# A new column layout for the transposed query weights in an agent-attention kernel with a gated convolution

## The chip, the cores and the metric

The kernel runs on one core of one Trainium2 chip. The metric is the device time of one execution in microseconds (us). The engines are called PE (TensorE, with PEld for its weight loads), DVE (VectorE), ACT (ScalarE), POOL (GpSimd) and SP (SyncE, which here issues nearly all DMAs); the profile names them so.

## The reference

Attention through 49 "agents", and on its output a gated causal convolution with two projections. There are 4 batches of N = 12800 rows with C = 128 channels, all in float32.

```
a2k     = softmax(scale * agents @ k.T)        # 49 x N
agent_v = a2k @ v                              # 49 x 128
q2a     = softmax(scale * q @ agents.T)        # N x 49
x       = q2a @ agent_v                        # N x 128
gate    = sigmoid(sum over 5 taps: conv_w[tap] * x[row - 4 + tap])
out     = ((gate * (x @ w_val)) @ w_out)
```

## The kernel before

The kernel never forms x. With the 49 query weights of a row as input, the convolution and the value projection are linear, so agent_v, conv_w and w_val are folded into small stationary matrices (`fold_weights`, five steps per batch: normalise, scale, subtract, transpose, split), one per tap for the gate and one for the values.

**Units and chunks.** A batch is cut into 10 units of 1280 rows and into 25 chunks of 512. Per unit, `key_scores`, `agent_values` and `queries` run; per chunk, `gates`, `values` and `project`.

**Precision.** Matmuls on the transposed weights run in f16. To keep float32 accuracy each weight w and each stationary value s is held as a high part and a rest (w = w_hi + w_lo, s = s_hi + s_lo), and the products hi*hi, lo*hi and hi*lo are added up by contraction over partitions: the columns of one matmul carry several copies of the 49 weights. 49 low parts, 49 high parts and 30 of the high parts once more (to meet the rests of s) fill 128 columns. The other 19 high parts that have to meet rests of s have no column left; they go into a second tile, x2.

**From weights to x1.** `queries` ends with `qw` (128 rows x 10 blocks x 49 weights, float32; L772). ACT casts it to the high parts (L779), POOL copies 30 of them again (L784) and subtracts to get the low parts (L794); all land in `pt` (128 x 10 x 128, f16). Then `transposes` turns `pt` around: for the first four units on PE (L849) with copies by ACT and DVE (L856, L861), for the other 36 by a DMA transpose (L835) that SP issues. The result is a half of an `x1` tile: 128 partitions (one per column of `pt`) by 2560 positions, two units to a tile, with the last four positions of the tile before in front of it (`halo`, on POOL, L816 and L819).

**From x1 to x2.** `shifts` (L884) copies 19 partitions of x1 into x2, each five times, shifted by 0 to 4 positions (the taps): 95 partitions. It does so by two transfers of SP's queue, one of 15 rows that lie three partitions apart and one of 4 neighbours; once per unit for the first four units, later once for two units (5 KB a row). For each chunk, `gates` runs five matmuls on x1 (one per tap, L922) and one on x2 (L926); `values` runs one on x1 (L949) and one on x2 (L953); then `project` runs three (L992 to L994). Between them stand a tanh on ACT (L935), a product on DVE (L962, `h`), the split of `h` on ACT (L968, `hh`) and POOL (L973, `hl`), and the scaled output on ACT (L1006).

**Order.** Every step is entered into a `Plan` with an engine, an estimated duration and its keys for reading and writing. PE runs in the order that a text written out by hand gives (`order`); the other engines' order, SP's queue among them, comes out of a list scheduling with the estimated durations. So each engine works in a fixed order, and a late step holds up all that stands behind it on its engine. Loads of k, q and v go through 11 buffers (`ld`), outputs through 4 (`ob`), `pt` through 4, x1 through 4 and x2 through 3.

The names of the layout before are these:

```
THREES = 15
NDUP = 2 * THREES
X2R = 19
X2CUTS = ((0, THREES, 3, 0.5), (THREES, X2R, 1, 0.3))
```

## Time and profile before

| | us |
|---|---|
| three timed runs | 424.02, 425.49, 425.74 |
| their median | 425.49 |
| span of the profiled execution (first to last instruction) | 423.6 |
| PE busy in it | 403.9 (95%) |
| ACT, DVE, POOL busy | 301.5, 293.3, 228.2 |
| mean granted clock of PE | 0.985 |

The profile is that of an execution of its own, whose time stands in the table only as its span; what lies around the span (the start and the end of an execution) and the spread from run to run make up the difference to the runs. In its rows a line such as L922 is a line of the kernel above, `out<-in` are the names of tiles without their numbers, so that `x` stands for x1 and x2 alike: `x<-pt` is the transpose into x1, `x<-x` the pair of transfers from x1 into x2. A wait names who waited, and for whom.

### The profile page before, as it was taken

What the parts mean: (1) busy time and instruction counts of PE and PEld (TensorE: products, weight loads), DVE (VectorE), ACT (ScalarE), POOL (GpSimd) and SP (SyncE); (2) the same over time, 40 slices, a digit from 0 to 9 for tenths busy, and PEclk for the clock granted to TensorE, in tenths of its full rate; (3) what the DMA queues carried; (4) which work ended last, traced back from release to release, by engine and by line L of the source; (5) the groups of instructions that cost most, each with busy time, mean ns of one, the idle gap of its engine ahead of it and who ended that gap; (6) DMA issues with size and microseconds to landing.
All of it is one profiled execution on the core that took longest, in us unless ns stands there. A gap on an engine that the chain in (4) does not pass through costs nothing.

```text
span 423.6 us, 10042 instructions
## 1 busy us (share of the span) xinstructions
PE 403.9 (95%) x3907; PEld 197.0 (47%) x3907; DVE 293.3 (69%) x562; ACT 301.5 (71%) x521; POOL 228.2 (54%) x263
## 2 busy tenths in 40 slices
PE   4979999999999999999999899999999989999995
PEld 1358434346555443446555343335555534344443
DVE  3757899867875978667795575767765678676231
ACT  1564568779966777678876486778876567788776
POOL 1002557654657565554566355574366277877553
PEclk9969999999999999999999899999999999999998
DMA  8999999999999999999999999999999977755733
GB/s 320 420 417 411 370 367 353 301 295 310 412 293 283 346 317 362 304 278 356 351 379 324 271 299 370 314 332 302 296 393 322 239 196 161 199 163 176 205 121 124
DMA packets 75129, 127.62 MB, mean 301 GB/s; under 512 B 50466, under 2 KB 50850, under 8 KB 75084
## 3 DMA queue, kind: packets, MB, share of 16 engines
q1 hardware_dynamic: 74940, 126.87, 96.9%
q8 instruction: 30, 0.49, 0.5%
q10 hardware_dynamic: 144, 0.13, 0.2%
q14 instruction: 15, 0.12, 0.1%
HBM read 79.25 MB, written 26.21 MB: 249 GB/s over the span
## 4 chain that ended last, share of the span: by engine, by line
PE 78%; DMA 9%; DVE 8%; ACT 1%; POOL 1%; issue 1%; SPq 0%; POOLq 0%; DVEq 0%; ACTq 0%
PE gate L922 23%; PE sc L376 17%; PE av L480 10%; PE val L949 5%; PE out L992 5%; PE val L953 5%; PE gate L926 5%; PE out L993 4%; DMA ld<-kT 4%; PE out L994 4%; DMA x<-pt 3%; DMA x<-x 2%; DVE h L962 1%; DVE qw L772 1%; DVE qsm L763 1%
## 5 line engine op out<-in xcount | busy, mean ns | idle before, releaser
L973 POOL TENSOR_TENSOR hl<-h,hh 128x512 f16<-128x512 f32 (+1 forms) x101 | 116.9, 1158 | 96.1 <-ACT hh L968 96.0
L922 PE MATMUL gate<-x,stat 128*128 128x512 f16 (+1 forms) x500 | 125.2, 380 | 0.2 <-ACT th L935 0.2
L962 DVE SCALAR_TENSOR_TENSOR h<-th,val 128x512 f32<-128x512 f32 x100 | 67.8, 678 | 66.8 <-PE out L993 26.2
L376 PE MATMUL sc<-ld,ag_sb 128*32 128x320 f32 x1280 | 101.5, 447 | 7.6 <-DMA ld<-kT 7.0
L935 ACT ACTIVATE th<-gate,unscale 128x512 f32<-128x512 f32 x100 | 68.3, 683 | 33.3 <-PE gate L926 31.7
L1006 ACT ACTIVATE ob<-out,oscale 128x512 f32<-128x512 f32 x98 | 67.3, 687 | 21.3 <-PE out L994 20.1
L922 PEld LDWEIGHTS <-stat 128*128 128x128 f16 x505 | 46.3, 97 | 63.7 <-issue 14.8
L968 ACT CAST hh<-h 128x512 f16<-128x512 f32 (+1 forms) x101 | 61.5, 609 | 17.2 <-DVE h L962 16.4
L750 POOL TENSOR_TENSOR qw<-sT,qmx 128x490 f32<-128x490 f32 x40 | 41.4, 1035 | 47.6 <-DVE qmx L745 47.5
L376 PEld LDWEIGHTS sc<-ld,ag_sb 128*32 128x32 f32 x1280 | 36.7, 111 | 59.4 <-issue 25.7
L480 PE MATMUL av<-ld,eT 128*32 128x129 f32 (+1 forms) x1400 | 50.7, 279 | 1.0 <-DVE eT L386 1.0
L480 PEld LDWEIGHTS av<-ld,eT 128*32 128x32 f32 (+1 forms) x1400 | 47.1, 117 | 7.5 <-issue 2.5
L794 POOL TENSOR_TENSOR pt<-qw,pt 128x490 f16<-128x490 f32 x40 | 44.8, 1120 | 3.1 <-ACT pt L779 2.9
L471 ACT ACTIVATE e<-ks,kbias 128x320 f32<-128x320 f32 x80 | 39.3, 554 | 5.4 <-DVE eT L386 3.3
L386 DVE STREAM_TRANSPOSE sT<-sc 128x640 f32<-128x640 f32 x40 | 33.6, 839 | 13.4 <-PE sc L376 12.7
L402 ACT COPY ks<-sc 128x640 f32<-128x640 f32 x40 | 27.7, 691 | 21.2 <-PE sc L376 19.1
L386 DVE STREAM_TRANSPOSE eT<-e 128x640 f32<-128x640 f32 x40 | 33.5, 842 | 9.8 <-ACT e L471 5.2
L926 PE MATMUL gate<-x,stat 95*128 95x512 f16 x100 | 38.3, 383 | 1.5 <-DMA x<-x 1.5
L949 PE MATMUL val<-x,stat 128*128 128x512 f16 x100 | 38.2, 382 | 0.8 <-DVE h L962 0.6
L953 PE MATMUL val<-x,stat 95*128 95x512 f16 x100 | 38.1, 381 | 0.0
L994 PE MATMUL out<-hl,wo 128*128 128x512 f16 x98 | 37.0, 378 | 1.1 <-POOL hl L973 1.1
L992 PE MATMUL out<-hh,wo 128*128 128x512 f16 x98 | 37.3, 381 | 0.1
(130 smaller groups left out, 389.4 us busy)
## 6 DMA issues: line engine op xcount, KB each, us to landing
ld<-kT SPq DMA_DIRECT2D x40, 640.0 KB
ld<-qT SPq DMA_DIRECT2D x40, 640.0 KB
ld<-vP SPq DMA_DIRECT2D x39, 645.0 KB
outT<-ob SPq DMA_DIRECT2D x48, 512.0 KB
x<-x SPq DMA_DIRECT2D x18, 375.0 KB
x<-x SPq DMA_DIRECT2D x18, 100.0 KB
outT<-ob SPq DMA_DIRECT2D x3, 256.0 KB
x<-x SPq DMA_DIRECT2D x4, 187.5 KB
```

What stands on the lines that cost most here:

```text
L376: nc.tensor.matmul(out=out[g * BLK : (g + 1) * BLK, j, 0:GT], lhsT=ag_sb[:, b, j * BLK : (j + 1) * BLK], rhs=src[:, g * GT : (g + 1) * GT] ...
L386: nc.vector.transpose(out=out.rearrange("p n (j i) -> p j n i", j=2), in_=in_.rearrange("p j (n i) -> p j n i", i=BLK),)
L480: nc.tensor.matmul(out=av[o + j : o + j + cols, 0 : C + 1], lhsT=et[:, n, j : j + cols], rhs=vt[:, n, :], start=(u == 0 and n < 2), stop=( ...
L922: nc.tensor.matmul(out=pg, lhsT=stat[:, k, :], rhs=x1[:, c : c + w], start=(k == 0), stop=False,)
L926: nc.tensor.matmul(out=pg, lhsT=stat[0 : TAPS * X2R, TAPS + 1, :], rhs=x2[0 : TAPS * X2R, o2 : o2 + w], start=False, stop=True,)
L935: lambda: nc.scalar.activation(out=th, in_=pg, func=AF.Tanh, scale=unscale[:, 0:1]),
L949: nc.tensor.matmul(out=pv, lhsT=stat[:, TAPS, :], rhs=x1s[(b * NCH + n0 // CH) // 5 % NX][:, PAD + o2 : PAD + o2 + w], start=True, stop=False,
L953: nc.tensor.matmul(out=pv, lhsT=stat[0 : TAPS * X2R, TAPS + 2, :], rhs=x2[0 : TAPS * X2R, o2 : o2 + w], start=False, stop=True,)
L962: lambda: nc.vector.scalar_tensor_tensor(out=h, in0=th, scalar=1.0, in1=pv, op0=ALU.add, op1=ALU.mult),
L968: "act", 0.16 + 0.42 * scale, lambda: nc.scalar.copy(out=hh, in_=h),
L973: lambda: nc.gpsimd.tensor_tensor(out=hl, in0=h, in1=hh, op=ALU.subtract),
L1006: lambda: nc.scalar.activation(out=ob[:, o : o + w], in_=po, func=AF.Copy, scale=oscale),
```

## The change

The columns of `pt` get a new layout. The high parts lie first at every fourth column: of columns 32 to 99, column 32 + 4i + r holds weight 16r + i for r = 0, 1, 2 and i = 0 to 16 (weights 16 and 32 stand there twice); the fourth slot, r = 3, holds a second copy of 16 of the weights, and column 99 is the first of 17 low parts. The other 32 low parts fill columns 0 to 31, and columns 116 to 127 hold 12 more second copies. x2 then takes its 19 rows from partitions 32, 36, ..., 92 (16 rows) and 85, 89, 93 (3 rows), and fills its own partitions 24 to 118; its other partitions are set to zero once, and the matmuls on x2 read all 128 partitions instead of 95. The stationary matrices are laid out to match.

On the engines this means:

- ACT writes the high parts with a step of four columns, 510 elements a row instead of 490 (two weights twice).
- POOL writes the second copies by two instructions (160 and 120 elements) instead of one (300), and the low parts by two (320 and 170) instead of one (490).
- In `fold_weights` the rests are made by five subtractions (values: three before, gate: four before), and ACT copies the high parts by four instructions instead of two.
- Three instructions on POOL clear x2 at the start.
- The estimates in the plan change a little (ACT 0.58 to 0.6; POOL 0.44 to 0.5 and 1.09 to 1.15), so that some steps change places.

PE's instructions keep their order. On DVE, the value part of the first batch's fold before (`wst` is the folded matrix, `sT` the next unit's transposed scores):

```order
L597 TENSOR_SCALAR wst_124<-val,rs 128x49
L582 SCALAR_TENSOR_TENSOR wst_124<-val,rs,wst_124 128x30
L582 SCALAR_TENSOR_TENSOR wst_124<-val,rs,wst_124 128x15
L582 SCALAR_TENSOR_TENSOR wst_124<-val,rs,wst_124 128x4
L386 STREAM_TRANSPOSE sT_86<-sc_135 128x2x10x32
```

and the same place on DVE in the changed kernel:

```order
L640 TENSOR_SCALAR wst_124<-val,rs 128x3x17
L624 SCALAR_TENSOR_TENSOR wst_124<-val,rs,wst_124 128x16
L624 SCALAR_TENSOR_TENSOR wst_124<-val,rs,wst_124 128x12
L624 SCALAR_TENSOR_TENSOR wst_124<-val,rs,wst_124 128x2
L624 SCALAR_TENSOR_TENSOR wst_124<-val,rs,wst_124 128x16
L624 SCALAR_TENSOR_TENSOR wst_124<-val,rs,wst_124 128x3
L406 STREAM_TRANSPOSE sT_86<-sc_135 128x2x10x32
```

Two subtractions more stand ahead of `sT`. On POOL, at the weights of units 18 and 19 (`pt_99` and `pt_100`) before:

```order
L794 TENSOR_TENSOR pt_99<-qw_91,pt_99 128x10x49
L973 TENSOR_TENSOR hl_117<-h_111,hh_114 128x512
L794 TENSOR_TENSOR pt_100<-qw_92,pt_100 128x10x49
L784 TENSOR_SCALAR pt_100<-qw_92 128x10x30
L750 TENSOR_TENSOR qw_90<-sT_86,qmx_88 128x490
L973 TENSOR_TENSOR hl_118<-h_112,hh_115 128x512
```

and there now:

```order
L821 TENSOR_TENSOR pt_99<-qw_91,pt_99 128x10x32
L826 TENSOR_TENSOR pt_99<-qw_91,pt_99 128x10x17
L1006 TENSOR_TENSOR hl_117<-h_111,hh_114 128x512
L821 TENSOR_TENSOR pt_100<-qw_92,pt_100 128x10x32
L826 TENSOR_TENSOR pt_100<-qw_92,pt_100 128x10x17
L813 TENSOR_SCALAR pt_100<-qw_92 128x10x16
L813 TENSOR_SCALAR pt_100<-qw_92 128x10x12
L777 TENSOR_TENSOR qw_90<-sT_86,qmx_88 128x490
L1006 TENSOR_TENSOR hl_118<-h_112,hh_115 128x512
```

Each instruction on `pt` has become two; the steps stand in the same order. On SP, the same units' transposes and their pair of transfers into x2 (here `x_105`, from `x_1_102`) before:

```order
L835 DMA_TRANSPOSE x_1_102<-pt_99 128x10x128
L369 DMA ld_71<-kT 128x1280
L835 DMA_TRANSPOSE x_1_102<-pt_100 128x10x128
L1021 DMA outT<-ob_123 128x1024
L369 DMA ld_61<-kT 128x1280
L369 DMA ld_62<-qT 128x1280
L884 DMA x_105<-x_1_102 75x1x2560
L884 DMA x_105<-x_1_102 20x1x2560
```

and now:

```order
L869 DMA_TRANSPOSE x_1_102<-pt_99 128x10x128
L389 DMA ld_71<-kT 128x1280
L869 DMA_TRANSPOSE x_1_102<-pt_100 128x10x128
L1054 DMA outT<-ob_123 128x1024
L389 DMA ld_61<-kT 128x1280
L389 DMA ld_62<-qT 128x1280
L917 DMA x_105<-x_1_102 80x1x2560
L917 DMA x_105<-x_1_102 15x1x2560
```

Nothing has moved there; the pair is cut 80 and 15 instead of 75 and 20. On SP, places are changed at one earlier spot (an output and a load) and within the work for units 23 to 29; on POOL and ACT at several, mostly the two parts of `pt` against each other and against `hl`.

The core of the diff:

```diff
-THREES = 15
-NDUP = 2 * THREES
+HI = 32
+FOURS = 17
+RUN = 16
+LO1 = HI + 4 * FOURS - 1
+TWICE = 12
 X2R = 19
-X2CUTS = ((0, THREES, 3, 0.5), (THREES, X2R, 1, 0.3))
+X2O = 24
+X2CUTS = ((0, RUN, HI, 0.5), (RUN, X2R, HI + 53, 0.3))
+
+
+def highs(x):
+
+
+    if len(x.shape) == 2:
+        return x[:, HI : HI + 4 * FOURS].rearrange("p (i r) -> p r i", r=4)
+    return x[:, :, HI : HI + 4 * FOURS].rearrange("p k (i r) -> p k r i", r=4)
+
+
+def overlapped(x):
+
+    ap = [tuple(d) for d in x.ap]
+    return bass.AP(x.tensor, x.offset, ap[:-1] + [(RUN, 3), (1, FOURS)])
...
+    for t in x2s:
+        nc.gpsimd.memset(t, 0.0)
...
-        def rest(out, full, s, hi):
-            dve.scalar_tensor_tensor(
-                out=out, in0=full, scalar=rs[:, s : s + 1], in1=hi,
-                op0=ALU.mult, op1=ALU.subtract,
-            )
...
+            less(pick(out, slice(HI + 3, HI + 4 * RUN, 4)), pick(full, slice(2 * RUN + 1, A)), pick(hi, 2, slice(1, FOURS)))
+            less(pick(out, slice(P - TWICE, P)), pick(full, slice(RUN + 1, RUN + 1 + TWICE)), pick(hi, 1, slice(1, 1 + TWICE)))
+            less(pick(out, slice(HI + 4 * RUN, HI + 4 * RUN + 2)), pick(two, slice(0, 2), 0), pick(hi, slice(1, 3), 0))
+            less(x2_(slice(0, RUN)), pick(full, slice(0, RUN)), pick(hi, 0, slice(0, RUN)))
+            less(x2_(slice(RUN, X2R)), pick(full, slice(2 * RUN - 3, 2 * RUN)), pick(hi, 1, slice(RUN - 3, RUN)))
...
+            nc.scalar.copy(
+                out=wg[:, :, 0:HI].rearrange("p k (r i) -> p k r i", i=RUN), in_=hi[:, :, 0:2, 0:RUN]
+            )
+            nc.scalar.copy(out=wg[:, :, LO1 : LO1 + FOURS], in_=hi[:, :, 2, :])
...
-        add(
-            "act", 0.58, lambda: nc.scalar.copy(out=pt[:, :, A : 2 * A], in_=w),
+        hi = highs(pt)
+        add(
+            "act", 0.6, lambda: nc.scalar.copy(out=hi[:, :, 0:3], in_=overlapped(w)),
             [("qw", g % NPT)], [(*p_, 0)],
         )
...
+        def again():
+            for to, a0, n in ((pt[:, :, HI + 3 : HI + 4 * RUN : 4], 2 * RUN + 1, RUN), (pt[:, :, P - TWICE :], RUN + 1, TWICE)):
+                nc.gpsimd.tensor_scalar(
+                    out=to, in0=w[:, :, a0 : a0 + n], scalar1=1.0, scalar2=0.0,
+                    op0=ALU.mult, op1=ALU.add,
+                )
+
+        add("pool", 0.5, again, [("qw", g % NPT)], [(*p_, 2)])
+
+        def lows_():
+            nc.gpsimd.tensor_tensor(
+                out=pt[:, :, 0:HI].rearrange("p n (r i) -> p n r i", i=RUN),
+                in0=w[:, :, 0:HI].rearrange("p n (r i) -> p n r i", i=RUN),
+                in1=hi[:, :, 0:2, 0:RUN], op=ALU.subtract,
+            )
+            nc.gpsimd.tensor_tensor(
+                out=pt[:, :, LO1 : LO1 + FOURS], in0=w[:, :, HI:A], in1=hi[:, :, 2, :],
+                op=ALU.subtract,
+            )
+
+        add("pool", 1.15, lows_, [("qw", g % NPT), (*p_, 0)], [(*p_, 1)])
...
-        for r0, r1, every, us in X2CUTS:
-            first = A + (2 if every == 3 else 3 * THREES)
-            rows = x1[first : first + 1 + (r1 - r0 - 1) * every : every, c : c + 1]
+        for r0, r1, first, us in X2CUTS:
+            rows = x1[first : first + 1 + (r1 - r0 - 1) * 4 : 4, c : c + 1]
             view = [rows.ap[0], (1, TAPS), (1, n * UNIT)]
             add(
                 "dma", 0.6,
                 lambda r0=r0, r1=r1, rows=rows, view=view: nc.sync.dma_start(
-                    out=x2[r0 * TAPS : r1 * TAPS, o : o + n * UNIT],
+                    out=x2[X2O + r0 * TAPS : X2O + r1 * TAPS, o : o + n * UNIT],
...
             nc.tensor.matmul(
-                out=pg, lhsT=stat[0 : TAPS * X2R, TAPS + 1, :],
-                rhs=x2[0 : TAPS * X2R, o2 : o2 + w], start=False, stop=True,
+                out=pg, lhsT=stat[:, TAPS + 1, :], rhs=x2[:, o2 : o2 + w],
+                start=False, stop=True,
             )
...
             nc.tensor.matmul(
-                out=pv, lhsT=stat[0 : TAPS * X2R, TAPS + 2, :],
-                rhs=x2[0 : TAPS * X2R, o2 : o2 + w], start=False, stop=True,
+                out=pv, lhsT=stat[:, TAPS + 2, :], rhs=x2[:, o2 : o2 + w],
+                start=False, stop=True,
             )
```

77 lines of the change are left out of this document (30 added, 47 removed).

## The prediction

> **What bounds the kernel now.** I read the page first, then who waits for whom on the matmul engine, then busy time by stretches, the chain of work that ended last, the DMA views and last the groups of instructions by shape. The page's first lines, and from the busy times by stretches two spans of the run:
>
> ```profile
> span 423.6 us, 10042 instructions
> PE 403.9 (95%) x3907; PEld 197.0 (47%) x3907; DVE 293.3 (69%) x562; ACT 301.5 (71%) x521; POOL 228.2 (54%) x263
> 60.00:412.00 352.00, 348.57 (x3295) 164.52 (x3294) 249.28 (x467) 265.15 (x458) 209.38 (x230) 1.00 1.00 293
> ```
>
> In the third row the columns are the stretch, its length, and busy time of PE, PEld, DVE, ACT and POOL, then the granted clock, the DMA share and GB/s. From 60 to 412 us TensorE is idle for 352.00 - 348.57 = 3.4 us. So a change off TensorE can win back about that, plus what an idle gap costs afterwards, and no more. The waits of TensorE in that stretch (who, for whom, us in total, times, longest):
>
> ```profile
> PE gate L926 <- DMA x<-x: 1.5, 1, 1.5
> PE out L994 <- POOL hl L973: 1.1, 1, 1.1
> PE val L949 <- DVE h L962: 0.6, 1, 0.6
> ```
>
> The first is the one that the change touches: `x<-x` is the pair of transfers that fills x2, and L926 the matmul that reads x2. It waits once in the whole run. The chain of work tells where, with start, duration and what:
>
> ```profile
> 220.73 7.50 DMA x<-pt
> 228.28 7.34 DMA x<-x
> 236.89 2.24 PE gate L922 x5
> ...
> 243.56 1.19 PE gate L922 x5
> ```
>
> A transpose by DMA (`x<-pt`) is followed at once by the pair, which lands at 228.28 + 7.34 = 235.62, and TensorE goes on. But its next five gate matmuls take 2.24 us, against 1.19 seven microseconds later. The stretches around it show why:
>
> ```profile
> 234.00:236.00 2.00, 0.51 (x3) 0.21 (x3) 1.05 (x3) 0.32 (x1) 0.10 (x1) 1.00 0.66 137
> 237.00:240.00 3.00, 3.00 (x8) 1.03 (x7) 1.99 (x7) 0.96 (x2) 1.65 (x3) 0.50 1.04 327
> 240.00:243.00 3.00, 3.00 (x34) 1.56 (x36) 2.24 (x9) 1.67 (x4) 0.76 (x3) 0.93 0.96 310
> ```
>
> After 1.5 us of idle TensorE the granted clock is 0.50 for 3 us and 0.93 for the next three: 3 x 0.50 + 3 x 0.07 = 1.7 us of matmul work lost while TensorE counts as busy. This one wait costs 1.5 + 1.7 = 3.2 us.
>
> [...]
>
> **What the change does to the transfers.** The pair still moves 95 rows of 5 KB; only which partitions are read and written changes (15 rows three apart plus 4 neighbours become 16 rows four apart plus 3, and the target moves from partitions 0-94 to 24-118). What the DMA engines do with such packets shows where nothing else runs. First a stretch with loads alone (6 to 14 us), then one in which one pair is the only transfer until its end (398.58 to 401.65 us); the second row of each is packets, MB and the share of 16 engines:
>
> ```profile
> DMA packets 735, 3.35 MB, mean 419 GB/s; under 512 B 80, under 2 KB 80, under 8 KB 735
> q1 hardware_dynamic: 735, 3.35, 101.4%
> ```
>
> ```profile
> DMA packets 112, 0.49 MB, mean 158 GB/s; under 512 B 17, under 2 KB 17, under 8 KB 112
> q1 hardware_dynamic: 112, 0.49, 56.1%
> ```
>
> Loads: 1.014 x 16 x 8 us over 735 - 80 = 655 big packets is 0.198 us each. The pair: 0.561 x 16 x 3.07 us over 112 - 17 = 95 packets is 0.290 us each, though no other transfer is there. So the packets of the pair hinder each other, and what differs from a load is which partitions they touch. Best case: 95 x 0.198 / 16 = 1.2 us for what takes 3.07 now; worst case: no change. I take 2.2 us, about half way, since the writes still fall on rows that are close together, so 0.9 us is gained on a pair with nothing beside it.
>
> [...]
>
> Under load the gain comes with a second one. The DMA engines are full between 60 and 340 us, and SyncE is held while it pushes. The queue between 60 and 340 us:
>
> ```profile
> q1 hardware_dynamic: 55788, 90.06, 107.7%
> ```
>
> Two pushes of transposes (start, duration):
>
> ```profile
> 212.77 7.23 SPq L835 DMA_TRANSPOSE x<-pt  x1
> 220.73 2.63 SPq L835 DMA_TRANSPOSE x<-pt  x1
> ```
>
> And one late in the run, with little traffic:
>
> ```profile
> 392.53 1.66 SPq L835 DMA_TRANSPOSE x<-pt  x1
> ```
>
> A push that takes 1.66 us when there is room took 7.23 here, and the second transpose, on which the pair waits, could start only after it. The pair before this one lies in that queue, so its gain arrives here as well: another 0.9 us at most, 0.5 taken. Needed are 1.5 us. I count 0.9 + 0.5, plus the 0.5 us by which TensorE comes later from the start (below), less 0.4 for the later copy on POOL, if none of it hides behind the held queue: 1.5 to 1.9. So the wait just goes, and with it the half clock: **-3.2 us**. Bounds: 0 if the pair gets no faster; above zero it is +0.7, the largest later copy, since no other step ahead of the pair grows.
>
> The second wait of TensorE (1.1 us, for POOL `hl`) has a DMA behind it too; in order of time, in brackets the idle time ahead and what ended it:
>
> ```profile
> 338.78 0.19 POOL L819 COPY x<-x 128x4 f16<-128x4 f16 x1 [5.99 <-DMA x<-pt]
> ```
>
> ```profile
> 340.13 0.38 PE L994 MATMUL out<-hl,wo 128*128 128x512 f16 x1 [1.11 <-POOL hl L973]
> ```
>
> That copy (the halo) waits 6.0 us until a transpose has landed, and the `hl` for which TensorE waits stands behind it on POOL. A less full DMA queue brings that forward a little: **-0.3 us**, between 0 and -1.1.
>
> **What it adds on the other engines.** Rows by shape (count, busy us, mean ns, idle before):
>
> ```profile
> L973 POOL TENSOR_TENSOR hl<-h,hh 128x512 f16<-128x512 f32 x99 | 115.5, 1168 | 94.8 <-ACT hh L968 94.7
> L973 POOL TENSOR_TENSOR hl<-h,hh 128x256 f16<-128x256 f32 x2 | 1.3, 671 | 1.3 <-ACT hh L968 1.3
> L794 POOL TENSOR_TENSOR pt<-qw,pt 128x490 f16<-128x490 f32 x40 | 44.8, 1120 | 3.1 <-ACT pt L779 2.9
> L784 POOL TENSOR_SCALAR pt<-qw 128x300 f16<-128x300 f32 x40 | 18.2, 457 | 20.6 <-DVE qw L772 20.6
> L616 POOL TENSOR_TENSOR wst<-gs,wst 128x75 f16<-128x75 f32 x3 | 1.1, 403 | 0.5 <-ACT wst L637 0.5
> L750 POOL TENSOR_TENSOR qw<-sT,qmx 128x490 f32<-128x490 f32 x40 | 41.4, 1035 | 47.6 <-DVE qmx L745 47.5
> L779 ACT CAST pt<-qw 128x490 f16<-128x490 f32 x40 | 23.9, 600 | 10.7 <-DVE qw L772 10.7
> L271 POOL MEMSET wst<- 128x256 f16 x2 | 0.6, 312 | 0.0
> L922 PE MATMUL gate<-x,stat 128*128 128x512 f16 x495 | 124.5, 381 | 0.2 <-ACT th L935 0.2
> L926 PE MATMUL gate<-x,stat 95*128 95x512 f16 x99 | 38.0, 384 | 1.5 <-DMA x<-x 1.5
> ```
>
> - POOL, per unit: L973's two sizes give 1.94 ns an element plus 174 ns. One subtraction of 490 (1120) becomes 320 and 170 elements: 795 + 504 = 1299. L616, which reads and writes with a step, takes 403 for 75 elements where that line gives 320, a quarter more: 1299 x 1.26 = 1637. One copy of 300 becomes two of 160 and 120: one more fixed cost, 0.17 as above. Together +0.35 to +0.7 us; I take 0.45, nearer to L973, which has L794's long rows. Forty units make 18 us on an engine that is busy 228 of 424: cover enough. Without that cover it is the slow rival below.
> - ACT, per unit: 510 instead of 490 elements, so 600 x 510 / 490 = 624 at most if the fixed part grew too. No row shows ACT writing every fourth element; a subtraction on POOL loses a quarter to its step (above), so the other end is +0.15. I take +0.02. ACT is idle for 29%.
> - Matmuls that read 95 rows (L926) last 384 ns, those that read 128 (L922) 381: filling up x2 costs nothing there.
> - Clearing three x2 at the start: 2560 columns, ten times the 312 ns of L271, 3 x 3.1 = 9.4 us on POOL. The first L750 has a long idle time ahead of it, so this is hidden; without that cover TensorE would wait up to 9 us:
>
> ```profile
> 35.26 1.02 POOL L750 TENSOR_TENSOR qw<-sT,qmx 128x490 f32<-128x490 f32 x1 [32.94 <-DVE qmx L745]
> ```
>
> The folding of the weights is longer: five subtractions for three on DVE for the value weights, five for four for the gate weights, and four copies for two on ACT. In the first batch this is where TensorE does wait. From the order of time around 44 to 52 us:
>
> ```profile
> 44.33 0.53 DVE L582 SCALAR_TENSOR_TENSOR wst<-val,rs,wst 128x30 f16<-128x30 f32 x3
> 44.77 0.84 DVE L386 STREAM_TRANSPOSE sT<-sc 128x640 f32<-128x640 f32 x1
> ...
> 52.07 0.72 PE L849 MATMUL sc<-ident,pt 128*128 128x128 f16 x10 [0.52 <-DVE sT L386]
> ```
>
> Three subtractions take 0.53, so two more take 0.35; `sT` stands right behind them on DVE, and DVE's row goes on to the next `sT`, for which TensorE waits at 52.07. POOL's subtractions beside it (five for four) and the first longer copy do not add to that wait but can outlast it. I take **+0.5 us** (0.2 to 0.9; a gain is excluded, since instructions only come in). In the later batches TensorE has other work then; only the fold at 345 us has a wait near it (L949, 0.6): **+0.1 us** (0 to 0.7).
>
> Sum: -3.2 - 0.3 + 0.5 + 0.1 = -2.9 us. On the profiled span of 423.6 that is 420.7. The runs took 424.02 to 425.74 with a median of 425.49, 1.9 over the span (start and end of an execution, and spread between runs); I carry the difference over: 425.5 - 2.9 = **422.6 us**.
>
> **The rivals.** (1) The pair lands no sooner. [...] Against it: the pair alone takes 0.290 us a packet. Then the wait and the half clock stay, and only the costs count: 425.5 + 0.5 + 0.1 = 426.1, up to 426.8 if the later copies push the wait out by 0.7. [...]
>
> (2) Slower: POOL comes late with `hl`. TensorE's last projection matmul (L994) waits for `hl`, which would queue behind the longer copies. The work comes in bursts, and POOL is fullest here (the row's fifth busy time):
>
> ```profile
> 360.00:380.00 20.00, 20.00 (x115) 8.29 (x117) 13.74 (x25) 16.45 (x29) 17.03 (x18) 1.00 0.70 192
> ```
>
> It is busy 17.0 of 20 us. Forty units in some 350 us are two to three in such a stretch, so 18 to 19 then; it is full from 1.0 us more a unit on, and that is where this rival decides. If `hl` is late by 0.4 us in half of the ten units of the last batch that is 2 us, and one gap of 1.5 us brings a half clock again, 1.7: 425.5 + 0.6 + 2 to 3.7 = 428.1 to 429.8, with the wait for the pair still there (without it the case ends at 424.9 to 426.6, among the unchanged).
>
> (3) More comes free: the wait at 340 us goes whole (-1.1) and the costs at the start stay at their low end: 425.5 - 3.2 - 1.1 + 0.2 = 421.4, or 420.6 with the rest of the 3.4 us of idle time (0.8) as well.
>
> **How the numbers follow.** Forecast 0.47, no sooner 0.27, slower 0.17, more 0.09. The forecast's own range is 421.6 to 424.2, from the bounds of its terms (a part of the wait left over at the upper end). From 420.6 to 427.6 the range takes in these, the first rival and the last, and leaves out the second, 0.17. A measurement of this kernel tells about 0.5% from no change, which is 2.1 us: below 423.4 is faster. Most of the forecast and all of the last case lie there, 0.53; the rest of the forecast and most of the first rival are the same, 0.30; the second rival is slower, 0.17.
>
> **What would show it.** In the profile after: the packets of a lone pair at 0.20 to 0.25 us instead of 0.290; no wait of the x2 matmul for a DMA, and a granted clock of 1.00 from 237 to 240 us; POOL busy at 243 to 256 us; TensorE some 0.5 us later at 60 us. Wrong would be: the pair as slow as before (rival 1), or TensorE waiting for POOL `hl` in many places after 340 us (rival 2).

## The result, and the profile after

The changed kernel takes **430.57 us** (median of 8 runs, 428.97 to 431.38). The kernel before took 425.97 in 8 runs beside it. The ratio is **1.0089, 95% interval 1.0061 to 1.0118**: 0.9% slower. (The quotient of the two medians is 1.0108, inside that interval; every ratio in this text is the one on record, with its interval.) The forecast was 422.6, and the time lies above its range of 420.6 to 427.6.

The first lines of the page of the kernel after (span; busy time of each engine):

```profile
span 428.2 us, 10150 instructions
PE 403.3 (94%) x3907; PEld 196.0 (46%) x3907; DVE 299.3 (70%) x573; ACT 327.4 (76%) x529; POOL 256.1 (60%) x347
```

TensorE runs the same 3907 matmuls. ACT is busy for 25.9 us more (301.5 before), POOL for 27.9 more. The groups of the kernel after, by shape, name the places (mean of one is the number ahead of the second bar):

```profile
L807 ACT CAST pt<-qw 128x510 f16<-128x510 f32 x40 | 56.8, 1427 | 13.2 <-DVE qw L799 12.8
L821 POOL TENSOR_TENSOR pt<-qw,pt 128x320 f16<-128x320 f32 x40 | 35.8, 896 | 12.8 <-ACT pt L807 12.4
L813 POOL TENSOR_SCALAR pt<-qw 128x160 f16<-128x160 f32 x40 | 23.0, 574 | 25.0 <-DVE qw L799 22.5 <-PE gate L959 1.7 <-PE out L1026 0.7
L826 POOL TENSOR_TENSOR pt<-qw,pt 128x170 f16<-128x170 f32 x40 | 22.8, 569 | 0.0
L813 POOL TENSOR_SCALAR pt<-qw 128x120 f16<-128x120 f32 x40 | 11.8, 294 | 0.0
L959 PE MATMUL gate<-x,stat 128*128 128x512 f16 x99 | 37.5, 379 | 0.0
```

The cast of `pt` took 600 ns for 490 elements and takes 1427 for 510. (Forty times this difference is 33 us, and ACT's total grew by less: in the profile the row of an instruction can begin before the one ahead of it has ended; the cast at 58.96 us lasts 1.46 and the next row of ACT begins at 60.14.) POOL's four pieces add up to 2.33 us a unit, against 1.58. POOL now waits 12.4 us for the cast, where it waited 2.9. L959, the matmul that reads x2, no longer waits for a DMA: that part came as forecast. Who TensorE does wait for, in the kernel after:

```profile
PE sc L883 <- POOL pt L826: 2.6, 2, 1.4
PE gate L955 <- ACT th L968: 2.2, 7, 0.8
```

Both are new in this size (0.2 us each before). Two stretches, of the kernel before first (length, then busy time of PE, PEld, DVE, ACT, POOL, then clock and DMA):

```profile
40.00:70.00 30.00, 28.02 (x293) 12.70 (x289) 26.64 (x62) 18.69 (x33) 17.72 (x25) 1.00 1.02 367
70.00:412.00 342.00, 338.57 (x3210) 159.99 (x3203) 239.62 (x449) 256.76 (x444) 203.06 (x223) 1.00 0.99 291
```

The same of the kernel after, and the place where the half clock was, and the stretch in which POOL is fullest:

```profile
40.00:70.00 30.00, 24.85 (x263) 11.18 (x264) 24.73 (x61) 18.54 (x30) 16.88 (x31) 1.00 0.97 365
70.00:412.00 342.00, 336.89 (x3207) 158.78 (x3206) 242.36 (x461) 278.91 (x449) 223.21 (x296) 1.00 0.94 289
237.00:240.00 3.00, 2.99 (x17) 1.60 (x16) 1.20 (x4) 1.95 (x3) 2.67 (x4) 1.00 0.91 274
360.00:380.00 20.00, 19.66 (x112) 7.98 (x109) 13.93 (x25) 17.06 (x25) 17.96 (x26) 1.00 0.57 166
```

Between 40 and 70 us TensorE works 3.2 us less than before, and between 70 and 412 another 1.7 less (the granted clock from 20 to 40 us, which bears on the first stretch, as e_order shows below, is 0.83 in both profiles), although the wait for x2 and its half clock (0.50 from 237 to 240 us before, 1.00 now) are gone from there. The first wait for POOL's `pt`, with the chain that leads to it, in order of time:

```profile
39.29 1.40 ACT L807 CAST pt<-qw 128x510 f16<-128x510 f32 x1 [2.19 <-DVE qw L799]
40.77 0.87 POOL L821 TENSOR_TENSOR pt<-qw,pt 128x320 f16<-128x320 f32 x1 [0.77 <-ACT pt L807]
41.61 0.56 POOL L826 TENSOR_TENSOR pt<-qw,pt 128x170 f16<-128x170 f32 x1
42.22 0.73 PE L883 MATMUL sc<-ident,pt 128*128 128x128 f16 x10 [1.26 <-POOL pt L826]
```

The weights are ready at 39.29; ACT casts them, POOL waits 0.77 us for that cast and then subtracts twice, and TensorE waits 1.26 us for POOL. The cast is half of that chain.

### The profile page after: what moved, and what is told of

Read it like the earlier page. It is cut to its first block, busy times and chain, and to the rows that moved or that the text cites. A ratio compares the mean times of both kernels' runs of the same rounds, so it can differ in the third digit from the quotient of the medians.

```text
span 428.2 us, 10150 instructions
## 1 busy us (share of the span) xinstructions
PE 403.3 (94%) x3907; PEld 196.0 (46%) x3907; DVE 299.3 (70%) x573; ACT 327.4 (76%) x529; POOL 256.1 (60%) x347
## 4 chain that ended last, share of the span: by engine, by line
PE 56%; DVE 15%; ACT 13%; POOL 7%; DMA 4%; issue 4%; SPq 0%; POOLq 0%; DVEq 0%; ACTq 0%
PE gate L955 16%; PE sc L396 11%; PE av L500 9%; ACT pt L807 4%; DMA ld<-kT 4%; PE out L1025 3%; PE val L982 3%; PE out L1026 3%; PE val L986 3%; PE gate L959 3%; PE out L1027 3%; DVE h L995 3%; DVE qw L799 2%; ACT th L968 2%; POOL pt L821 2%
## 5 line engine op out<-in xcount | busy, mean ns | idle before, releaser
L807 ACT CAST pt<-qw 128x510 f16<-128x510 f32 x40 | 56.8, 1427 | 13.2 <-DVE qw L799 12.8
L821 POOL TENSOR_TENSOR pt<-qw,pt 128x320 f16<-128x320 f32 x40 | 35.8, 896 | 12.8 <-ACT pt L807 12.4
L813 POOL TENSOR_SCALAR pt<-qw 128x160 f16<-128x160 f32 x80 | 27.5, 434 | 25.0 <-DVE qw L799 22.5
L959 PE MATMUL gate<-x,stat 128*128 128x512 f16 x100 | 37.8, 378 | 0.0
```

The lines of the kernel that those rows point to most:

```text
L807: "act", 0.6, lambda: nc.scalar.copy(out=hi[:, :, 0:3], in_=overlapped(w)),
L959: nc.tensor.matmul(out=pg, lhsT=stat[:, TAPS + 1, :], rhs=x2[:, o2 : o2 + w], start=False, stop=True,)
```

## The experiments

Each ratio is against the kernel before, timed beside it, with its 95% interval. Theory A: the cast on ACT, which writes every fourth column in three passes, makes the loss; the transfers are a gain as forecast. Rivals: B, POOL's longer work; C, the longer fold of the weights or another order of the planner; and, once more, that the transfers gain nothing.

| run | what it is | ratio | interval |
|---|---|---|---|
| e_dma | before + new transfers | 0.9895 | 0.9863 to 0.9928 |
| e_act | before + a row of 0.8 us of cast ahead of the cast | 1.0035 | 1.0003 to 1.0068 |
| e_pool | before + POOL's longer work | 1.0028 | 0.9999 to 1.0056 |
| e_three | these three together | 0.9972 | 0.9951 to 0.9994 |
| e_order | after, cast in column order | 0.9934 | 0.9909 to 0.9960 |
| e_start | e_order, old cast in units 0 to 3 | 0.9971 | 0.9947 to 0.9996 |
| e_late | e_order + POOL copy in the chain | 1.0090 | 1.0056 to 1.0123 |
| e_half | e_order + 0.56 us cast behind the cast | 0.9975 | 0.9951 to 0.9999 |
| e_load | e_order + 0.93 us cast behind the cast | 1.0108 | 1.0078 to 1.0139 |
| e_flat | e_order + 0.92 us cast without a step | 1.0185 | 1.0146 to 1.0224 |
| e_bload | before + the second cast of e_load | 1.0068 | 1.0040 to 1.0096 |
| e_fold | e_order, fold in column order too | 0.9936 | 0.9911 to 0.9960 |
| e_plain4 | no steps, 13 + 6 rows four apart | 1.0004 | 0.9977 to 1.0031 |
| e_plain3 | no steps, 16 rows three apart + 3 | 0.9939 | 0.9906 to 0.9971 |

**The parts alone.** First the transfers, on the old columns, so that x2 gets other rows than its weights belong to. Of each edit the core is shown, and `...` marks lines that are left out:

```
+X2CUTS = ((0, 16, 32, 0.5), (16, X2R, 85, 0.3))
...
-        for r0, r1, every, us in X2CUTS:
-            first = A + (2 if every == 3 else 3 * THREES)
-            rows = x1[first : first + 1 + (r1 - r0 - 1) * every : every, c : c + 1]
+        for r0, r1, first, us in X2CUTS:
+            rows = x1[first : first + 1 + (r1 - r0 - 1) * 4 : 4, c : c + 1]
```

> The kernel before with the new transfers alone: 16 rows four partitions apart and 3 more, x2 on partitions 24 to 118 and cleared at the start, x2's matmuls over 128 rows. The columns stay as they were, so x2 gets other rows than its weights belong to (that part of the computation is changed). Theory A (the transfers give what was forecast, and the cast on ACT takes more than that away again): 3 us less than the kernel before, ratio 0.990 to 0.995, no wait of the x2 matmul for a DMA and no half clock around 237 us. Theory C (the transfers themselves, or the order that the planner then finds, are worse): 1.000 or above, with new waits of TensorE for a DMA.

It gave 0.9895: 1.05% of 425.5 is 4.5 us, between 3.1 and 5.8, against the 3.5 of the two terms in the forecast. TensorE's waits for `hl` and for the pair in it, and where the second of them is:

```profile
PE out L996 <- POOL hl L975: 0.9, 1, 0.9
PE gate L928 <- DMA x<-x: 0.5, 1, 0.5
49.63 0.38 PE L928 MATMUL gate<-x,stat 128*128 128x512 f16 x1 [0.49 <-DMA x<-x]
```

The wait of 1.5 us for the pair at 235 us is gone, and so is the half clock behind it (1.00 from 237 to 240 us). The 0.5 us is another wait, at 49.63 us, where the kernel before has none. Of the 1.1 for `hl` 0.9 is left. So the gain was there, and the whole loss of the change is near 2% (1.0089 / 0.9895 = 1.0196, 8 us).

Next one more cast on ACT, ahead of the cast of `pt`:

```
+            nc.scalar.copy(
+                out=idle16[:, :, 0:68].rearrange("p n (i r) -> p n r i", r=4)[:, 0:5, 0:3],
+                in_=bass.AP(w.tensor, w.offset, [tuple(w.ap[0]), (A, 5), (16, 3), (1, 17)]),
+            )
             nc.scalar.copy(out=pt[:, :, A : 2 * A], in_=w)
```

> The kernel before with one more cast on ACT ahead of each unit's cast of pt: 255 elements into scratch, written at every fourth column, which took 812 ns in the weights' fold of the kernel after. So ACT's part of the pt chain grows from 600 to about 1410 ns, as in the kernel after (1427), and all else stays. Theory A (the long cast makes the loss): ratio 1.008 to 1.015, since the whole loss beside a gain of 3 us would be some 7 us. Theory B (the longer work on POOL makes it): 1.000 to 1.003.

And POOL's longer work alone (the subtraction in columns 0 to 31 and 32 to 48, and a copy of 42 columns, which stands in the part left out):

```
...
+            for a0, a1 in ((0, 32), (32, A)):
+                nc.gpsimd.tensor_tensor(
+                    out=pt[:, :, a0:a1], in0=w[:, :, a0:a1], in1=pt[:, :, A + a0 : A + a1],
+                    op=ALU.subtract,
+                )
```

> The kernel before with POOL's work on each unit lengthened to what the kernel after shows: the subtraction in two pieces of 32 and 17 columns, and one more copy of 420 elements into scratch, some 0.7 us a unit (1.58 us before, 2.33 after). ACT's cast stays at 600 ns. Theory A: ratio 1.000 to 1.004, POOL waits less for ACT than it now does. Theory B (POOL's longer work makes the loss): 1.008 to 1.015, with waits of TensorE for POOL pt or hl.

Neither is near 1.02: 1.0035 and 1.0028, the second not told from no change. Theory A had asked for 1.008 or more, so it had failed in this form. But e_act had not lengthened ACT's work as far as it meant to. Its first unit:

```profile
38.22 0.81 ACT L781 CAST idle<-qw 128x255 f16<-128x255 f32 x1 [2.19 <-DVE qw L773]
38.76 0.68 ACT L785 CAST pt<-qw 128x490 f16<-128x490 f32 x1
```

The second row begins 0.54 us after the first. From the start of the one to the end of the other are 1.22 us, where the changed kernel's cast takes 1.43, and ACT is busy for 322.0 us in all, where the changed kernel has 327.4. All three edits together (e_dma's, e_act's and e_pool's lines in one kernel):

> The kernel before with three parts at once, each of which has run alone: the new transfers (x2 gets other rows than its weights belong to, so that part of the computation is changed), the long cast on ACT (one more of 255 elements into scratch) and the longer work on POOL (two subtractions, one more copy of 420 elements into scratch). The fold and the columns of pt stay as before. If the three add up: 0.9895 x 1.0035 x 1.0028 = 0.996. Theory D (ACT and POOL stand in one chain, so that together they cost far more than each): 1.004 to 1.010, near the kernel after. Theory C (the missing part is in the fold or the order): about 0.996.

0.9972: the parts add up (0.9957 expected) and do not reach 1.0089; ACT and POOL in one chain do not cost far more together than each alone. What they had imitated was not all of it (ACT has 321.7 us here), and only an edit to the changed kernel itself could tell why.

**How the cast writes.** The next kernel copied a tile into scratch at the start, in ten forms, here (4) and (5):

```
+        go(src([(64, 10), (1, 3), (4, 16)], pout), src([(49, 10), (16, 3), (1, 16)]))
+        go(src([(64, 10), (4, 16), (1, 3)], pout), src([(49, 10), (1, 16), (16, 3)]))
```

> The kernel before with copies of one tile into scratch at the start, ten forms in this order on ACT twice, then on DVE and on POOL: (1) 480 elements, contiguous, f32 to f16; (2) 480, every second f16 written; (3) 480, three of every four f16 written in order, source contiguous; (4) 480, every fourth f16 written, three passes (the form of the kernel after); (5) the same places as in (4) but written in the order of the columns, source stepping by 16; (6) target contiguous, source stepping by 16; (7) 640, target contiguous, source in overlapping runs of four; (8) as (4) with an f32 target; (9) as (4) with every second f16; (10) as (4) with every eighth f16. Theory A1 (the distance between written elements costs, from 8 bytes on): (1), (2), (6), (7), (9) about 0.6 to 0.8 us on ACT, (4), (10) about 1.4, (5) and (3) in between or as (4). Theory A2 (what costs is the source's step of 64 bytes or the short runs): (5), (6) slow and (4) fast. Theory A3 (only f16 written in part costs): (8) fast where (4) is slow.

ACT's copies in order of time (start, duration); the first is contiguous, the second form (4), the third form (5), the last form (10). ACT ran all ten twice, with durations that agree to 0.01 us:

```profile
3.90 0.60 ACT L284 CAST pout<-qw 128x480 f16<-128x480 f32 x1 [1.48 <-DVE pout L278]
5.92 1.25 ACT L284 CAST pout<-qw 128x480 f16<-128x480 f32 x1
7.19 0.74 ACT L284 CAST pout<-qw 128x480 f16<-128x480 f32 x1
11.01 2.32 ACT L284 CAST pout<-qw 128x480 f16<-128x480 f32 x1
```

The same 480 places cost 1.25 us in three passes of every fourth column and 0.74 in the order of the columns. Every second f16 cost 0.78, every eighth 2.32; an f32 target with the same step in elements 1.04; a source with a step of 16 and a contiguous target 0.73. So A1 holds for the f16 targets, and (5) costs no more than its source's step does alone: what counts there is how far apart two writes are that follow each other. The distance in bytes does not explain all: 16 bytes apart took 2.32 us in f16 and 1.04 in f32, and no run has an f32 target without a step beside it.

That gives an edit of the changed kernel that touches nothing but the order of writing inside one instruction:

```
-            "act", 0.6, lambda: nc.scalar.copy(out=hi[:, :, 0:3], in_=overlapped(w)),
+            "act", 0.6, lambda: nc.scalar.copy(
+                out=pt[:, :, HI : HI + 4 * FOURS].rearrange("p n (i r) -> p n i r", r=4)[:, :, :, 0:3],
+                in_=bass.AP(w.tensor, w.offset, [tuple(w.ap[0]), (A, NBLK), (1, FOURS), (RUN, 3)]),
+            ),
```

> The kernel after, with the same elements of pt written by the same cast on ACT, but in the order of the columns (17 groups of three) instead of three passes that write every fourth column. On the scratch tile 480 elements took 743 ns in this order and 1245 in three passes, so the cast should take 790 ns instead of 1427; nothing else changes. Theory A (the write order of this cast is the main cost): 0.992 to 0.998 against the kernel before, most of the way from 1.009 to the 0.9895 of the transfers alone; the waits of TensorE for POOL pt at 42 and 54 us shrink by 0.6 us each, those for ACT th go. Theory B (POOL's longer work, which stays): 1.003 to 1.006. Theory C (the fold's longer instructions at the start or the planner's order): 1.005 to 1.009.

**0.9934**: faster than both kernels. Its cast, and its two stretches:

```profile
L807 ACT CAST pt<-qw 128x510 f16<-128x510 f32 x40 | 31.4, 788 | 14.3 <-DVE qw L799 14.0
```

```profile
40.00:70.00 30.00, 27.78 (x289) 12.28 (x288) 27.23 (x63) 19.15 (x34) 18.36 (x31) 1.00 1.02 377
70.00:412.00 342.00, 339.70 (x3221) 161.53 (x3220) 243.02 (x460) 264.53 (x455) 224.15 (x295) 1.00 0.96 290
```

639 ns less in one instruction a unit is worth 1.0089 / 0.9934 = 1.0156, 6.6 us. TensorE works 2.9 us more between 40 and 70 us and 2.8 more after that than in the changed kernel. Not all of the 2.9 is the cast's. From 20 to 40 us the granted clock differs between these two executions; here the changed kernel, e_order, and e_fold (below), which has the same cast as e_order:

```profile
20.00:40.00 20.00, 16.97 (x234) 14.86 (x234) 13.76 (x23) 12.30 (x24) 1.67 (x3) 0.83 1.02 416
20.00:40.00 20.00, 16.68 (x237) 12.85 (x229) 13.76 (x23) 11.90 (x24) 3.10 (x5) 0.91 1.02 414
20.00:40.00 20.00, 16.78 (x238) 14.87 (x234) 13.78 (x23) 12.19 (x24) 1.34 (x2) 0.83 1.02 415
```

and e_fold's first stretch:

```profile
40.00:70.00 30.00, 26.91 (x281) 12.07 (x278) 26.19 (x62) 17.83 (x32) 19.05 (x33) 1.00 1.02 374
```

At the clock of 0.83 the cast in order is worth 26.91 - 24.85 = 2.1 us there. The planner's costs, POOL's instructions and the fold are those of the changed kernel, so with the cast in order all that B and C still cost, and the 0.19 us that the cast is still longer than before, is what separates this kernel from the transfers alone: 0.4%, which the two intervals do not tell from nothing.

**Why 0.64 us cost so much.** At the start:

> The kernel after with the cast of pt in three passes (1427 ns) in the first four units only, whose transposes run on TensorE, and in the order of the columns in the other 36. In the profile of the kernel after TensorE waits there 2.6 us for POOL pt, in that of the ordered kernel 0.4. If the loss arises there: 0.9934 + 0.005 = 0.998 to 1.000; the other 36 units then hold the remaining 1.0 per cent. If the loss lies all in the later units: 0.993 to 0.995; if all in the first: 1.006 to 1.010.

```
+            if g < PE_FIRST:
+                nc.scalar.copy(out=hi[:, :, 0:3], in_=overlapped(w))
+                return
```

0.9971, so by the ratios 0.37% or 1.6 us arise in the first four units; the two intervals leave it just clear of nothing. Its first stretch is that of the changed kernel again, at the same clock of 0.83 from 20 to 40 us:

```profile
40.00:70.00 30.00, 25.00 (x264) 11.31 (x265) 24.72 (x61) 18.53 (x30) 16.99 (x30) 1.00 0.99 365
```

For the other 36 units, two kernels were to separate ACT's time from the length of the chain. The first puts a second cast behind the ordered one, for which nothing waits:

```
+            nc.scalar.copy(
+                out=idle16[:, :, 0:68].rearrange("p n (i r) -> p n r i", r=4)[:, 0:6, 0:3],
+                in_=bass.AP(w.tensor, w.offset, [tuple(w.ap[0]), (A, 6), (RUN, 3), (1, FOURS)]),
+            )
```

> The kernel after with the cast of pt in the order of the columns (780 ns, alone it gave 0.9934), and behind that cast one more on ACT, 306 elements into scratch with every fourth f16 written, for which nothing waits. ACT is busy as long as in the kernel after (about 1.4 us a unit), but the chain from the weights through ACT and POOL to the transposes stays 0.6 us shorter. Theory A1 (the loss comes from the chain's length): 0.993 to 0.997. Theory A2 (it comes from ACT's load: gate, ks, hh and out stand behind the cast): 1.003 to 1.010.

1.0108. The first stretch is unharmed here (27.65 us against e_order's 27.78, both with 0.91 from 20 to 40 us), and the loss comes after it, with more waits for `th`, the tanh that stands behind the casts on ACT:

```profile
40.00:70.00 30.00, 27.65 (x287) 12.45 (x287) 26.93 (x63) 20.80 (x36) 18.61 (x32) 1.00 1.02 375
70.00:412.00 342.00, 334.30 (x3186) 157.67 (x3183) 239.16 (x457) 281.30 (x481) 220.17 (x292) 1.00 0.97 288
```

```profile
PE gate L967 <- ACT th L980: 3.6, 8, 1.0
```

The second lengthens the chain and leaves ACT alone, but it gives POOL 24 us more (280.3 against 256.3):

```
         def lows_():
+            nc.gpsimd.tensor_scalar(
+                out=idle16[:, :, 0:50], in0=pt[:, :, HI : HI + 50], scalar1=1.0, scalar2=0.0,
+                op0=ALU.mult, op1=ALU.add,
+            )
```

> The kernel after with the cast of pt in the order of the columns, and between it and the subtractions one copy of 500 elements on POOL that reads what the cast wrote, some 0.5 to 0.6 us. The chain is about as long as in the kernel after, ACT's load is not. Theory A1 (the chain's length): 1.003 to 1.010. Theory A2 (ACT's load): 0.993 to 0.997, or 1.000 if POOL's own load, now 2.9 us a unit, begins to count.

1.0090. Here the first stretch is hit (24.90 us of TensorE, against e_fold's 26.91, both with 0.83 from 20 to 40 us), and later TensorE waits for POOL:

```profile
40.00:70.00 30.00, 24.90 (x264) 11.23 (x265) 24.69 (x61) 16.30 (x29) 19.25 (x34) 1.00 0.97 365
70.00:412.00 342.00, 336.15 (x3209) 159.05 (x3208) 244.93 (x461) 260.91 (x450) 245.24 (x332) 1.00 0.97 290
```

```profile
PE out L1035 <- POOL hl L1014: 2.0, 2, 1.3
```

So either costs about as much as the stepped cast did, and I had set them up as if only one could. In the first four units it is the chain: a second cast behind the first does no harm there. Later e_late does not tell the chain's length from POOL's own longer work, and the changed kernel's waits are those of e_load (`th`, 7 times) and not those of e_late (`hl`).

Three more kernels asked what in ACT's second cast costs. A row of about the same length without a step (920 ns against 930), against e_load:

```
-                out=idle16[:, :, 0:68].rearrange("p n (i r) -> p n r i", r=4)[:, 0:6, 0:3],
-                in_=bass.AP(w.tensor, w.offset, [tuple(w.ap[0]), (A, 6), (RUN, 3), (1, FOURS)]),
+                out=idle16[:, :, 0:87],
+                in_=bass.AP(w.tensor, w.offset, [tuple(w.ap[0]), (40, NBLK), (1, 87)]),
```

> As e_load, but the second cast on ACT writes 870 elements into scratch without a gap, which should take about as long (930 ns) as the 306 stepped ones. Theory A2 (ACT's time is what costs, not how it writes): 1.008 to 1.013 as e_load, with waits of TensorE for ACT th. Theory S (a stepped write slows other engines down): 0.994 to 1.000.

1.0185: without a step it costs no less, so it is not the stepped writing that harms the other engines; ACT's time does. That it costs more than forecast goes with ACT's total, which is 4.4 us above e_load's. Half of the stepped cast, against e_load (its source is cut in the same way):

```
-                out=idle16[:, :, 0:68].rearrange("p n (i r) -> p n r i", r=4)[:, 0:6, 0:3],
+                out=idle16[:, :, 0:68].rearrange("p n (i r) -> p n r i", r=4)[:, 0:3, 0:3],
```

> As e_load, with 153 instead of 306 elements in the second cast, so about half of its time on ACT beyond the fixed part. If the cost is proportional to ACT's time: 1.002 to 1.004 (half way between 0.9934 and 1.0108). If it only starts when ACT is nearly full (above some 325 us in all): 0.993 to 0.998.

0.9975. With ACT's busy time from the pages: 307.1 us (e_order) 0.9934, 319.8 (e_half) 0.9975, 332.7 (e_load) 1.0108, 337.1 (e_flat) 1.0185. The first 12.7 us cost 0.4%, the next 12.9 cost 1.3%, the last 4.4 cost 0.8% (within its interval the rate of the step before): a microsecond on ACT cost more here where ACT had more to do. e_three, built from the kernel before, fits in (321.7 us, 0.9972). The changed kernel has 327.4 us; on a straight line between e_half and e_load that gives an estimate of 1.0053, and with the 0.37% of the first four units 1.009, where 1.0089 was measured. The second cast of e_load behind the cast of the kernel before:

```
             nc.scalar.copy(out=pt[:, :, A : 2 * A], in_=w)
+            nc.scalar.copy(
+                out=idle16[:, :, 0:68].rearrange("p n (i r) -> p n r i", r=4)[:, 0:6, 0:3],
+                in_=bass.AP(w.tensor, w.offset, [tuple(w.ap[0]), (A, 6), (16, 3), (1, 17)]),
+            )
```

> The kernel before with the second cast of e_load (306 stepped elements into scratch) behind its own cast of pt. Theory A2 (ACT's time): 1.008 to 1.017 as the step from the ordered kernel to e_load. If it counts only together with POOL's longer work and the new transfers: 1.000 to 1.005, near the 1.0035 of the shorter second cast that ran ahead of the cast of pt.

1.0068 with ACT at 327.0 us, between the two forecasts, and a smaller step than from e_order to e_load. It still waits 2.4 us for `x<-x`, and such a wait can cover some of ACT's lateness; that is argued, not shown.

**The rest of the change.** The fold's high parts written in column order, in three places on DVE and ACT (`in_cols` and `cols` swap the two dimensions as in e_order):

```
-            dve.tensor_scalar_mul(vhi[:, 0:3], overlapped(pv[:, 0:A]), rs[:, 1:2])
+            dve.tensor_scalar_mul(in_cols(vhi), cols(pv[:, 0:A]), rs[:, 1:2])
-            dve.tensor_scalar_mul(ghi[:, :, 0:3], overlapped(gw), rs[:, 0:1])
+            dve.tensor_scalar_mul(in_cols(ghi), cols(gw), rs[:, 0:1])
-            add("act", 0.4, lambda: nc.scalar.copy(out=ghi[:, :, 0:3], in_=overlapped(gs)), ["gs"], [(*w_, "g")])
+            add("act", 0.4, lambda: nc.scalar.copy(out=in_cols(ghi), in_=cols(gs)), ["gs"], [(*w_, "g")])
```

> The kernel after with the cast of pt in the order of the columns, and the same for the three writes of the weights' high parts in the fold (ACT 255 elements, 812 ns in three passes, DVE 255 and 51 elements, 832 and 340 ns). Expected by the scratch copies: 812 becomes about 430 ns, and DVE's 832 about 560. If the fold holds a part of what separates the ordered kernel (0.9934) from the transfers alone (0.9895): 0.991 to 0.993, TensorE does not wait for POOL wst at 44 us. If it is hidden: 0.9934.

0.9936 against 0.9934: the stepped writes of the fold cost nothing that shows. Its added instructions were not tried alone.

Two kernels without any stepped write in the cast, with other rows for x2; the copies and the fold follow, and POOL gets one more short copy a unit (0.2 to 0.3 us):

```
-X2CUTS = ((0, THREES, 3, 0.5), (THREES, X2R, 1, 0.3))
+X2CUTS = ((0, 13, 49, 4, 0.4), (13, X2R, 51, 4, 0.3))
```

> A complete kernel that writes everything in runs as before (49 columns of the rests, 49 of the weights, 30 copies) and gets rows four apart by choosing others for x2: weights 0, 4, ... 48 (13 rows) and 2, 6, ... 22 (6 rows), to partitions 24 to 118. ACT's cast stays at 600 ns, POOL has one more copy (60 elements, some 0.2 us a unit). Theory A: 0.988 to 0.993, as the transfers alone. If the number of rows (16 and 3) matters for the transfers and not their distance: 0.995 to 1.000, with a wait of TensorE for x<-x.

```
-X2CUTS = ((0, THREES, 3, 0.5), (THREES, X2R, 1, 0.3))
+X2CUTS = ((0, 16, 49, 3, 0.5), (16, X2R, 93, 2, 0.3))
```

> As the last, with 16 rows three apart (weights 0, 3, ... 45) and 3 rows two apart (44, 46, 48). If the distance of four matters: 0.996 to 1.002, lone packets of x<-x near 290 ns as before and the wait for x<-x still there. If it is the number of rows (16 and 3 instead of 15 and 4) or the place in x2: 0.988 to 0.993, packets near 230 ns.

1.0004 and 0.9939. The first lies just above the range that was forecast if the number of rows matters, the second lies between its two forecasts. A pair with nothing beside it at the end of the run shows what each does; first the kernel after (from 402.60 to 404.95 us), then e_plain4 (399.34 to 402.66), then e_plain3 (396.99 to 400.21):

```profile
DMA packets 131, 0.49 MB, mean 209 GB/s; under 512 B 35, under 2 KB 35, under 8 KB 131
q1 hardware_dynamic: 131, 0.49, 59.5%
```

```profile
DMA packets 130, 0.49 MB, mean 147 GB/s; under 512 B 35, under 2 KB 35, under 8 KB 130
q1 hardware_dynamic: 130, 0.49, 41.6%
```

```profile
DMA packets 129, 0.49 MB, mean 151 GB/s; under 512 B 34, under 2 KB 34, under 8 KB 129
q1 hardware_dynamic: 129, 0.49, 57.2%
```

Worked out as in the prediction: 0.595 x 16 x 2.35 / 96 = 0.233 us a packet in the kernel after, 0.416 x 16 x 3.32 / 95 = 0.233 in e_plain4, 0.572 x 16 x 3.22 / 95 = 0.310 in e_plain3. The packet's time went with the distance of the rows here (four apart 0.233, three apart 0.310). The pair's time does not follow from it alone: at 0.233 us a packet the pair with 13 and 6 rows takes 3.3 us, that with 16 and 3 takes 2.35, and no view here shows how the packets are spread over the engines. TensorE's wait for the pair near 235 us went with the packet's time: 1.5 us before and none in e_dma, and in e_plain4 (first row) and e_plain3 (second row), with e_plain3's clock behind it:

```profile
233.69 0.39 PE L933 MATMUL gate<-x,stat 128*128 128x512 f16 x1 [0.30 <-DMA x<-x]
234.27 0.39 PE L933 MATMUL gate<-x,stat 128*128 128x512 f16 x1 [1.20 <-DMA x<-x]
237.00:240.00 3.00, 3.00 (x35) 1.61 (x37) 2.70 (x14) 2.11 (x4) 2.45 (x4) 1.00 0.95 275
```

So e_plain3 has no faster pair and keeps most of the wait, but not the half clock, and gains 0.6% all the same. e_plain4 has lost most of the wait and gains nothing; it waits 2.2 us for `hl` in two places. What makes the difference between these two is open.

## Why the prediction was wrong

- **The pair.** Right. Forecast 2.2 us alone and 0.20 to 0.25 us a packet; measured 2.35 and 0.233. (The 2.2 was a choice between two bounds; the rows written lie next to each other in all runs, so what that costs is not shown.) The wait at 235 us went and the clock stayed at 1.00. The two terms for the transfers, 3.5 us, lie within the 3.1 to 5.8 of e_dma. The first rival (the pair lands no sooner) fell with it. Less sure is the share of the half clock, 1.7 of the 3.2 us: it was counted as a consequence of the wait, and in e_plain3 a wait of 1.2 us at the same place was followed by a clock of 1.00.
- **The cast on ACT.** This step failed, and with it the sum, in which ACT has no term at all: "no row shows ACT writing every fourth element; a subtraction on POOL loses a quarter to its step, so the other end is +0.15. I take +0.02." Measured +0.83 us a unit, more than five times the upper end. The row behind that end was a subtraction of 75 elements on POOL, in which the fixed part is the larger one (174 of 320 ns, by the line through L973's two sizes). Its 403 - 320 = 83 ns over 75 elements are 1.1 ns each, and 510 of them would have been +0.56 us. A loss for each element was carried over as a share of an instruction.
- **ACT's cover.** "ACT is idle for 29%" was taken as cover for the cast. It isn't: the cast stands in the chain to the transposes (e_start, 1.6 us in four units), and ahead of `th` on ACT (e_load). From e_order, 25.6 us more on ACT cost 1.7%. Writing the same cast in column order, with nothing else changed, took the changed kernel from 1.0089 to 0.9934: that the cast made the loss is shown.
- **POOL.** Forecast +0.35 to +0.7 us a unit, +0.45 taken; measured +0.76, just above the upper end. The subtractions took 1465 ns, within 1299 to 1637. The copies took 868 instead of 457; one of them writes every fourth column, 574 ns for 160 elements against 294 for the other's 120. Alone this costs 0.28%, which can't be told from nothing.
- **The second rival** gave a slower kernel through POOL's `hl`. The kernel is slower, but in the kernel after the only wait for `hl` is 0.4 us at the very end. Its 428.1 to 429.8 us lie below the 430.57 measured, but near it, and that nearness is luck. No rival let ACT become late, and that was the one step without a row of its own.
- **`hl` at 340 us.** -0.3 forecast; in e_dma the wait fell by 0.2.
- **The start.** +0.5 forecast for the fold, between 0.2 and 0.9. TensorE's work between 40 and 70 us fell by 3.2 us in the kernel after. Among the profiles with a clock of 0.83 from 20 to 40 us, 1.1 of it are left once the cast is in order (28.02 before, 26.91 in e_fold); among those with 0.91 it is 0.35 (18.13 in e_dma, 17.78 in e_order, between 40 and 60 us). So the cast makes some 2.1 of the 3.2, and what is left for the fold and POOL's longer work together is about the size of the forecast; the runs do not part these two.
- **Matmuls over 128 rows and clearing x2.** Right: 379 ns against 384, and 6.6 us of clearing on POOL (9.4 forecast) that nothing waited for.

What stays open is how the loss after 70 us divides between ACT's time and the chain's length. The waits for `th` and the estimate from ACT's busy time speak for ACT's time; the one run for the chain, e_late, also made POOL's work longer.

## What to carry over

An operation that the trace does not show, on an engine that stands in a chain, deserves a rival of its own: measure it in scratch, or scale a loss seen in a short instruction by the element and not by the instruction (here +0.56 us by the element and +0.15 by the instruction, +0.83 measured). When a layout needs columns that are not neighbours, let the innermost dimension of the write run through neighbouring columns, and let the source take the step (the cast of `pt` took 1427 ns in passes and 788 in column order). Idle share of an engine is no cover for an instruction that others wait for (ACT was idle for 29%, and the 639 ns of its cast were worth 1.6%); ask what stands behind it on its queue.

## What was not expected of the hardware

- In p_step the distance between f16 writes that follow each other cost time on ACT, POOL and DVE. For 480 elements ACT took 0.60 us contiguous, 0.78 with every second f16 and 1.25 with every fourth, and 2.32 with every eighth; POOL took 0.59 and, with every fourth, 1.24; DVE 0.42 and 0.69. The same places in column order took ACT 0.74, and a contiguous target from a source with that step 0.73. With an f32 target and every fourth element, 16 bytes apart, ACT took 1.04, less than half of f16's 2.32 at the same distance.
- Pairs of transfers with rows four partitions apart moved packets of 5 KB in 0.233 us; where most rows lie three apart it was 0.290 (before) to 0.310 (e_plain3).
- The half clock early in the run (0.50 from 26 to 30 us in the kernel before and in the kernel after) differed between executions: of the profiles here, whatever the kernel, some show a granted clock of 0.83 from 20 to 40 us and some 0.91, and with the same cast in order TensorE then works 26.91 us (e_fold) or 27.78 us (e_order) between 40 and 70 us. Such stretches are compared at the same clock.
- A wait of TensorE of 1.50 us was followed by a granted clock of 0.50 (237 to 240 us) in the kernel before, one of 1.20 us at the same place by 1.00 in e_plain3.
